# Expert routing beside the matmuls: new reckoned times, a wider wait, a gate on the search, row tiles one by one

## Chip, cores and metric

One core of one Trainium2 chip. The metric is the device time of one launch in microseconds (us). Three runs of the kernel before took 701.67, 702.32 and 698.46 us; the median is 701.67.

## What is computed

The kernel takes a windowed attention with a few global rows (8 batches, 8 heads, 512 local and 32 global rows, head size 64), lays its output out as 4608 rows of 512, and puts these through a layer of 8 experts. The experts are the part that matters here:

```python
logits = x @ w_gate
flat = logits.flatten()
order = np.argsort(-flat)
for idx in order:
    tok, e = (int(idx) // E, int(idx) % E)
    if assigned[tok] >= 0 or counts[e] >= cap:
        continue
    assigned[tok] = e
    counts[e] += 1
for e in range(E):
    mask = assigned == e
    h = np.maximum(x[mask] @ w1[e], 0.0)
    out[mask] = h @ w2[e]
```

Each expert gets exactly 576 rows (`cap`). Which expert is full next, and which rows it gets, is known only after a search over all logits that are still open.

## The kernel before

**Stages.** Attention runs first and writes the rows `xd` to memory. Then phase 0 of the routing runs alone. From 247.2 us on, eight experts follow one another, in the order in which the routing finds them full.

**One expert** (`ffn`, line 1096). All products are done in three fp32r parts: high x high, high x low, low x high. Part H is 16 groups of 12 matmuls, 128x272 each, of the weights `w1h`/`w1l` with the rows `xh`/`xl` (line 1119). After each group ScalarE writes `hh` and VectorE the remainder `hl`. Part Y begins with `rest_out` (line 1086, the last 32 rows) and goes on with four tiles of 128 rows in `rows_out` (line 1077, 24 matmuls of 128x512 each). When `rest_out` has been issued, `mid[0]` is set to the number of the expert. Beside an expert the inputs of the next are made ready: `get_w1` and `get_w2` gather its weights (GpSimd, by `widx`), `get_x` gathers its rows (by `idx`), `split_w1`, `split_w2` and `trans_x` (line 956) split them into the high part (ScalarE) and the low part (VectorE). `trans_x` first turns a tile of 128 rows on TensorE. Weights of the next expert come into the same tiles, so half of w1 may be split only after `f` is 4, and the rest only after `mid`.

**One routing phase** (`phase`, line 736, with `setup` and `search`, line 679). `setup` makes the keys, then the search does eight turns. A turn counts with 18 small matmuls into `A`, scales by `ce` on VectorE, sums with two matmuls, finds the bound by a scan (`pm`), lowers (`lower`) and compares again (`cand`, which writes `G`). From the eighth scan come `widx` (the next expert) and, after a prefix sum and one-hot products, `idx` (its rows). Phase `ph` serves expert `ph`, and runs beside the experts before it. Phase 7 has no search.

**The planner.** The order on each engine's queue is set when the kernel is built, by reckoned times. `step(ns)` (line 1016) is called after each large matmul and moves TensorE's reckoned time `V.now` on. `Queue` (line 527) adds a cost to `V.busy`, the reckoned time at which VectorE is through, for each operation issued (line 548). `mm` (line 626) does the small matmuls: it moves `V.now`, and sets `V.busy` to at least a little after it. In `chain` (line 991) the phases are generators: each yields the reckoned time from which it may go on, or -1, at which waiting `hl` operations (`fill`, by `bubble`) are issued first. Before a small matmul that reads a VectorE result it yields `ready()`, which is `V.busy` and a margin, `HOP`. `step` takes the first entry of `todo` whose time has come and whose condition holds (the gathers, splits, turned tiles and scatters), lets the routing go on, and issues one waiting low part (`lows`) when VectorE is nearly through. Low parts wait for 900 ns (`LOW`) after their high part, those of row tiles for 1500 (`TURN`). `calm` is: fewer than two low parts waiting. At the end of an expert, what is not yet ready is waited for with steps of 120 ns and no matmul.

The reckoned time is used for nothing but the order: on the chip each instruction waits for its data by semaphores.

Of the kernel before, what the change touches and what calls it, by code (L numbers as in the profile page):

```python
# [510 lines left out]
TX = 22000  # L511
TW = 34000
AHEAD = 200
HOP = 400
SLACK = 100
PACE = 250
CU = 64
# [9 lines left out]
class Queue:  # L527


    def __init__(s, eng):  # L530
        s.eng = eng
        s.now = s.busy = 0.0

    def ready(s):
        return s.busy + HOP

    def pace(s):
        return s.busy - PACE
# [1 line left out]
    def __getattr__(s, name):  # L540
        op = getattr(s.eng, name)

        def issue(*args, **kw):
            aps = [x for x in list(args) + list(kw.values()) if hasattr(x, "dtype") and hasattr(x, "shape")]
            n = max(int(np.prod(x.shape[1:])) for x in aps)
            fast = name in ("tensor_scalar", "tensor_copy") or name == "tensor_tensor" and all(
                mybir.dt.size(x.dtype) == 2 for x in aps)
            s.busy = max(s.busy, s.now) + 150 + n * (2.1 if "scan" in name else 1.9 if name == "transpose" else 0.55 if fast else 1.05)
            return op(*args, **kw)  # L549
        return issue  # L550


class Routing:
# [69 lines left out]
    def begin_ps(s, ctx):  # L623
        s.ps = ctx.enter_context(s.tc.tile_pool(name="rps", bufs=1, space=PSUM))

    def mm(s, out, *args, ns=60, **kw):
        s.nc.tensor.matmul(out, *args, **kw)  # L627
        s.V.now += ns
        s.V.busy = max(s.V.busy, s.V.now + 200)

    def t(s, name, shape, dt=F32):
        return s.sb.tile([128] + shape, dt, name="r_" + name)
# [16 lines left out]
    def lower(s, P, it):  # L649

        y = s.t("z%d" % (it % 2), [34], BF16)
        s.V.scalar_tensor_tensor(y, s.x, P, s.dg[:, it - 1], op0=ALU.subtract, op1=ALU.add)
        s.x = y

    def key(s, j):
# [23 lines left out]
    def search(s):  # L679
        nc = s.nc  # L680
        for it in range(NIT):
            yield -1
            yield s.when
            A = s.ps.tile([128, 2, E], F32, name="R")
            for i in range(18):
                j, r = slice(2 * i, 2 * i + 2), 32 * (i % 4)
                g, o = (s.G[:, i].rearrange("p a b -> p (a b)"), s.oh[:, j]) if i < 17 else (s.one[:, :32], s.rem[:, :2])
                s.mm(A[r:r + 32], g, o, ns=20, start=(i < 4), stop=(i >= 14))
            p = s.ps.tile([128, 16, E], F32, name="R2")
            if it == 0:  # L690
                s.digits(slice(0, 34))
                s.x = s.y0
            ce = s.t("ce", [2, 16, E], F16)
            s.V.tensor_tensor(ce, A[:, :, None, :].to_broadcast([128, 2, 16, E]),
                              s.dk[:, :, :, None].to_broadcast([128, 2, 16, E]), op=ALU.mult)
            when = s.V.ready()
            yield -1
            yield when
            for k in range(2):
                s.mm(p, s.big, ce[:, k], start=(k == 0), stop=(k == 1))  # L700
            pm = s.t("pm%d" % (it % 2), [16 * E])
            s.V.tensor_tensor_scan(pm, p.rearrange("p a b -> p (a b)"), s.fin[:, it], 0.0, op0=ALU.max,
                                         op1=ALU.min)
            P = pm[:, 16 * E - 1:16 * E]
            if it < NIT - 1:
                s.lower(P, it + 1)
                s.cand(s.x, s.step2[:, it + 1])
        s.P = P.bitcast(I32)
# [27 lines left out]
    def phase(s, ph):  # L736
        nc = s.nc
        last = ph == E - 1
        S = s.t("S", [68], BF16)
        vs = s.ix.tile([128, 1], F32, name="vs")  # L740
        if not last:
# [15 lines left out]
        a = s.t("a", [34])  # L757
# [21 lines left out]
        p = s.ps.tile([128, 68], F32, name="R")  # L779
# [42 lines left out]
        rhs = s.rhs  # L822
# [15 lines left out]
        p = s.ps.tile([128, 64], F32, name="R2")  # L838
        for j in range(34):
            r = 32 * (j % 4)  # L840
            s.mm(p[r:r + 32], rhs[:, j // 2, :, :, j % 2].rearrange("p a b -> p (a b)"), ohl[:, j // 2, :, j % 2], ns=20, start=(j < 4),
                 stop=(j >= 30))
        if more and ph:
            pg = s.ps.tile([128, E], F32, name="R")
# [48 lines left out]
def experts(ctx, tc, A, xd, ident, rt, out):  # L893
# [62 lines left out]
    def trans_x(xg, t):  # L956
        n = sizes[t]
        flush(1)
        p = ps.tile([128, 4, 128], F32, name="H", bufs=3)
        for d in range(4):  # L960
            nc.tensor.transpose(p[:, d, :n], xg[t][:n, 128 * d:128 * d + 128], ident[:n, :n])  # L961
        q = slice(128 * t, 128 * t + n)
        if rt.beside:
            split(xh[:, :, q], xl[:, :, q], p[:, :, :n], V, TURN)
        else:
            nc.scalar.activation(xh[:, :, q], p[:, :, :n], AF.Copy)
            V.tensor_tensor(xl[:, :, q], p[:, :, :n], xh[:, :, q], op=ALU.subtract)
# [23 lines left out]
    def chain():  # L991
        for ph in range(1, E):
            if 1 < ph < E - 1:
                yield from rt.setup(slice(0, 34))
            yield from rt.phase(ph)

    routing = chain()

    def bubble():
        while fill:  # L1000
            fill.pop(0)()

    def at(tag, t, f, cond=None):
        todo.append((tag, t, cond, f))
# [11 lines left out]
    def step(ns):  # L1016
        V.now += ns
        for i, (tag, t, cond, f) in enumerate(todo):
            if t <= V.now and (cond is None or cond()):
                todo.pop(i)  # L1020
                f()
                break
        while not done[0] and V.now >= need[0]:
            v = next(routing, None)
            if v is None:
                done[0] = True
            elif v < 0:
                bubble()
            else:
                need[0] = v  # L1030
        if lows and lows[0][0] <= V.now and V.busy < V.now + AHEAD:
            lows.pop(0)[1]()
        if V.busy < V.now and (done[0] or need[0] > V.now + SLACK):
            bubble()
# [16 lines left out]
    def get_x(p):  # L1051
        flush()
        xg = load_x(p)
        for t in range(5):
            r = pool_op(1040, sizes[t] * 2048)
            at(f"x{p}", r + (900 if p == 1 else 0), lambda t=t: trans_x(xg, t), lambda: mid[0] == p - 1)

    def get_w2(p):
        flush()
# [17 lines left out]
    def rows_out(ph, t):  # L1077
        p = ps.tile([128, DM], F32, name="Y", bufs=3)
        q = slice(128 * t, 128 * t + 128)
        for f in range(8):  # L1080
            for k, (h, w) in enumerate(((hh, w2h), (hh, w2l), (hl, w2h))):
                nc.tensor.matmul(p, h[:, f, q], w[f], start=(f + k == 0), stop=(f + k == 9))  # L1082
                step(216)
        out_tile(ph, t, p)

    def rest_out(ph):
# [9 lines left out]
    def ffn(ph):  # L1096
        nxt = ph + 1
        t0 = V.now
        cur[0] = ph
        half = []  # L1100
        if nxt < E:
            at(f"g{nxt}", t0, lambda: get_w1(nxt, half), lambda: nxt in rt.widx and not pending(f"b{ph}"))
            at(f"h{nxt}", t0, lambda: get_x(nxt), lambda: nxt in rt.idx and (mid[0] == ph or V.now > t0 + TX))
            at(f"v{nxt}", t0, lambda: get_w2(nxt), lambda: mid[0] == ph and nxt in rt.widx and
               (not pending(f"h{nxt}") or V.now > t0 + TW))
        for f in range(8):
            if f == 4:
                force(f"b{ph}")
                half.append(True)
                if ph == E - 1:  # L1110
                    force("out")
                    nc.gpsimd.drain()
            for hf in range(2):
                q = slice(HF * hf, HF * hf + HF)
                p = ps.tile([128, HF], F32, name="H", bufs=3)
                fs = slice(128 * f, 128 * f + 128)
                for d in range(4):
                    for k, (w, x) in enumerate(((w1h, xh), (w1h, xl), (w1l, xh))):
                        nc.tensor.matmul(p, w[d][:, fs], x[:, d, q], start=(d + k == 0), stop=(d + k == 5))  # L1119
                        step(117)  # L1120
                nc.scalar.activation(hh[:, f, q], p, AF.Relu)  # L1121
                if hf:
                    nc.scalar.activation(h32[:, f], p[:, HF - 32:HF], AF.Relu)  # L1123
                while fill:
                    fill.pop(0)()
                fill.append(lambda p=p, f=f, q=q: V.scalar_tensor_tensor(
                    hl[:, f, q], p, 0.0, hh[:, f, q], op0=ALU.max, op1=ALU.subtract))

        while fill:
            fill.pop(0)()  # L1130
        force(f"w{ph}")

        for part in (0, 1, 2, 3, 4) if ph == E - 1 else (4, 0, 1, 2, 3):
            if part == 4:
                rest_out(ph)
            else:
                rows_out(ph, part)
        while nxt < E and (pending(f"g{nxt}", f"h{nxt}", f"a{nxt}", f"x{nxt}", f"v{nxt}") or lows or nxt not in raw1):
            step(120)
            bubble()  # L1140
# [127 lines left out]
```

## Time and profile before

| | |
|---|---|
| median of three runs | 701.67 us (698.46 to 702.32) |
| profiled execution | 703.93 us, span 702.0 us |
| TensorE (PE) busy | 651.6 us, 93% of the span |
| VectorE (DVE) busy | 460.5 us, 66% |
| ScalarE (ACT) busy | 308.9 us, 44% |
| GpSimd (POOL) busy | 247.8 us, 35% |
| chain that ended last | TensorE 88%, VectorE 5%, issue 3%, DMA 2% |

The span runs from the first to the last instruction; the execution's own time is 1.9 us more. Times in rows are us from the start of the span. A row in order of time has the start, the length, the engine, the line, the operation, out<-in, the shapes, the count, and in brackets the engine's idle time before it with what ended that. All VectorE operations of the planner have line 549 (the helper that records them), and its small matmuls line 627, so they are told apart by tile. Matmuls are pipelined: the length of one is longer than the step from one to the next.

### The profile page before, as it was taken

How to read it: one execution, taken by the hardware profiler on the slowest of the kernel's cores; microseconds unless marked ns; L12 is line 12 of the kernel's file. 1: busy time of each engine (PE TensorE's matmuls, PEld its weight loads, DVE VectorE, ACT ScalarE, POOL GpSimd, SP SyncE). 2: the span in 40 equal slices, each digit the busy share in tenths (PEclk: the TensorE clock that was granted, in tenths of full speed). 3: DMA queues.
4: the chain of work that ended last, by engine and by line, in shares of the span. 5: the costliest groups of instructions: out<-in, count | busy, mean ns of one | idle time of the engine just before them, and what ended most of it. 6: DMA issues, size and time to landing. Idle time of an engine off the chain costs nothing.

```text
span 702.0 us, 24724 instructions
## 1 busy us (share of the span) xinstructions
PE 651.6 (93%) x10364; PEld 547.5 (78%) x10364; DVE 460.5 (66%) x1765; ACT 308.9 (44%) x828; POOL 247.8 (35%) x313
## 2 busy tenths in 40 slices
PE   7878989889992799989999999999999999999996
PEld 6666767677781699769879878978987987988985
DVE  4678777777876787687767767767776764640510
ACT  5776767776840253233324334333333332641410
POOL 4686658766610410430241141152132034412001
PEclk9999999999995599989999999999999999999999
DMA  8676767776310530630361361343135045631001
GB/s 256 198 222 198 225 209 233 240 218 207 111 67 2 184 122 5 252 113 1 129 203 39 125 197 49 121 127 122 44 132 179 17 145 197 207 128 46 16 15 50
DMA packets 41119, 93.91 MB, mean 134 GB/s; under 512 B 5424, under 2 KB 28208, under 8 KB 36912
## 3 DMA queue, kind: packets, MB, share of 16 engines
q0 software_dynamic: 10240, 51.39, 21.1%
q1 hardware_dynamic: 30768, 40.95, 19.2%
q8 instruction: 81, 1.33, 0.8%
q14 instruction: 30, 0.25, 0.1%
HBM read 74.49 MB, written 17.83 MB: 132 GB/s over the span
## 4 chain that ended last, share of the span: by engine, by line
PE 88%; DVE 5%; issue 3%; DMA 2%; ACT 1%; SPq 0%; POOLq 0%; ACTq 0%
PE H L1119 28%; PE Y L1082 27%; PE T L90 11%; PE S L90 7%; PE O L90 7%; PE R L627 4%; PE H L961 3%; PE Y L1090 2%; DVE r_pm L549 1%; DMA xg<-xd,idx 1%; DVE r_G L549 1%; DMA mask<-in_mask_dram 1%; DMA qk<-in_qk_dram 1%; DVE r_ce L549 0%; DMA out_dram<-y,idx 0%
## 5 line engine op out<-in xcount | busy, mean ns | idle before, releaser
L1119 PE MATMUL H<-xh,w1h 128*128 128x272 f32 x512 | 153.3, 299 | 1.4 <-DVE hl L549 1.3
L1119 PE MATMUL H<-xh,w1l 128*128 128x272 f32 x512 | 150.0, 293 | 0.0
L1119 PE MATMUL H<-xl,w1h 128*128 128x272 f32 x512 | 149.6, 292 | 0.0
L971 POOL DMA_INDIRECT out_dram<-y,idx x40 | 42.5, 1062 | 199.7 <-ACT y L1070 111.3
L1121 ACT ACTIVATE hh<-H 128x272 fp32r<-128x272 f32 x128 | 50.9, 398 | 127.5 <-PE H L1119 115.7
L1082 PE MATMUL Y<-w2h,hh 128*128 128x512 f32 x256 | 103.5, 404 | 0.0
L1082 PE MATMUL Y<-w2l,hh 128*128 128x512 f32 x256 | 103.2, 403 | 0.0
L1082 PE MATMUL Y<-w2h,hl 128*128 128x512 f32 x256 | 103.0, 402 | 0.0
L1119 PEld LDWEIGHTS H<-xh,w1h 128*128 128x128 f32 x512 | 97.4, 190 | 3.4 <-DVE hl L549 2.5
L1119 PEld LDWEIGHTS H<-xl,w1h 128*128 128x128 f32 x512 | 97.4, 190 | 0.2
L1119 PEld LDWEIGHTS H<-xh,w1l 128*128 128x128 f32 x512 | 97.2, 190 | 0.2
L126 POOL COPY vw<-vw 32x650 f32<-32x650 f32 x96 | 69.3, 722 | 59.0 <-DMA vw<-in_vw_dram 37.2
L180 ACT ACTIVATE p<-p,nm 128x128 f32<-128x128 f32 x256 | 78.0, 396 | 8.1 <-DVE nm L175 8.1
L1070 ACT ACTIVATE y<-Y 128x512 f32<-128x512 f32 (+1 forms) x40 | 21.4, 535 | 119.9 <-PE Y L1082 87.2
L175 DVE CUSTOM_DVE_ANT_0 p<-S,mask 128x128 f32<-128x128 f32 x256 | 56.5, 286 | 25.3 <-PE S L90 24.4
L549 DVE SCALAR_TENSOR_TENSOR hl<-H,hh 128x272 fp32r<-128x272 f32 x128 | 54.8, 434 | 26.3 <-ACT h L1123 16.8
L90 PE MATMUL S<-qk 64*32 64x128 f32 (+2 forms) x2240 | 53.2, 294 | 9.4 <-issue 6.8
L549 DVE TENSOR_TENSOR w2l<-w2r,w2h 128x512 fp32r<-128x512 f32 x64 | 42.9, 683 | 23.8 <-ACT w2h L929 23.8
L913 POOL DMA_INDIRECT xg<-xd,idx x40 | 42.8, 1071 | 42.1 <-DVE idx L549 29.0
L1082 PEld LDWEIGHTS Y<-w2h,hh 128*128 128x128 f32 x256 | 48.2, 188 | 10.3 <-issue 1.2
L1082 PEld LDWEIGHTS Y<-w2h,hl 128*128 128x128 f32 x256 | 48.1, 188 | 9.7
L1082 PEld LDWEIGHTS Y<-w2l,hh 128*128 128x128 f32 x256 | 48.3, 188 | 9.4
(175 smaller groups left out, 1130.5 us busy)
## 6 DMA issues: line engine op xcount, KB each, us to landing
qk<-in_qk_dram SPq DMA_DIRECT2D x64, 204.0 KB, 3.7
vw<-in_vw_dram SPq DMA_DIRECT2D x64, 162.5 KB, 3.5
xd<-xs SPq DMA_DIRECT2D x28, 256.0 KB, 3.5
qk<-in_qk_dram SPq DMA_DIRECT2D x32, 200.0 KB, 3.8
xd<-xs SPq DMA_DIRECT2D x1, 1024.0 KB
xg<-xd,idx POOLq DMA_INDIRECT x40, 3.6
out_dram<-y,idx POOLq DMA_INDIRECT x40, 2.8
vw<-in_ve_dram SPq DMA_DIRECT2D x32, 16.2 KB, 3.4
```

The costliest lines, as they stand in the source:

```text
L90: s.last = op(o, w, x, **kw)
L126: copy(bv[32 * g:32 * g + 32], av[32 * g + 32:32 * g + 64])
L175: nc.vector.tensor_tensor_reduce(s.p[:, c, :], s.st[:, c, :], mask[:, c, :], -SCALE, BIG, ALU.add, ALU.min, s.nm[:, c:c + 1])
L180: nc.scalar.activation(s.p[:, c, :], s.p[:, c, :], AF.Exp, bias=s.nm[:, c:c + 1], scale=-1.0)
L549: return op(*args, **kw)
L627: s.nc.tensor.matmul(out, *args, **kw)
L913: nc.gpsimd.indirect_dma_start(out=dst, out_offset=None, in_=src, element_offset=off, in_offset=bass.IndirectOffsetOnAxis(ap=idx, axis=0))
L971: nc.gpsimd.indirect_dma_start(out=out4 if t == 4 else out, out_offset=bass.IndirectOffsetOnAxis(ap=rt.idx[ph][:, k:k + 1], axis=0), in_=y ...
L1070: nc.scalar.activation(y, p[:, :w], AF.Copy)
L1082: nc.tensor.matmul(p, h[:, f, q], w[f], start=(f + k == 0), stop=(f + k == 9))
L1119: nc.tensor.matmul(p, w[d][:, fs], x[:, d, q], start=(d + k == 0), stop=(d + k == 5))
L1121: nc.scalar.activation(hh[:, f, q], p, AF.Relu)
```

## The change

The reckoned costs change: a VectorE operation has 60 ns instead of 150 beside its elements (a scan 190, and `lower` 190 more), an H matmul 124 instead of 117, a Y matmul 230 instead of 216, the small matmuls 23, 90 and 17, and the time from a small matmul to VectorE is 150 or nothing instead of 200. The margin `HOP` becomes `s.hop`: 280 (`SOON`) for phases 0 and 1 and 800 from phase 2 on. A phase is begun only when `rest_out` of the expert two back has been issued; until then the chain yields every 300 ns of reckoned time. Before a waiting low part is issued, waiting `hl` operations are. A row tile is turned only when no low part is waiting.

```diff
-HOP = 400
+SOON = 280
+HOP = 800
...
+        s.hop = SOON
 
     def ready(s):
-        return s.busy + HOP
+        return s.busy + s.hop
...
-            s.busy = max(s.busy, s.now) + 150 + n * (2.1 if "scan" in name else 1.9 if name == "transpose" else 0.55 if fast else 1.05)
+            s.busy = max(s.busy, s.now) + (190 if "scan" in name else 60) + n * (
+                2.1 if "scan" in name else 1.9 if name == "transpose" else 0.55 if fast else 1.05)
...
-    def mm(s, out, *args, ns=60, **kw):
+    def mm(s, out, *args, ns=60, lag=150, **kw):
         s.nc.tensor.matmul(out, *args, **kw)
         s.V.now += ns
-        s.V.busy = max(s.V.busy, s.V.now + 200)
+        s.V.busy = max(s.V.busy, s.V.now + lag)
...
         s.V.scalar_tensor_tensor(y, s.x, P, s.dg[:, it - 1], op0=ALU.subtract, op1=ALU.add)
+        s.V.busy += 190
...
-                s.mm(A[r:r + 32], g, o, ns=20, start=(i < 4), stop=(i >= 14))
+                s.mm(A[r:r + 32], g, o, ns=23, lag=-50, start=(i < 4), stop=(i >= 14))
...
-                s.mm(p, s.big, ce[:, k], start=(k == 0), stop=(k == 1))
+                s.mm(p, s.big, ce[:, k], ns=90, start=(k == 0), stop=(k == 1))
...
         last = ph == E - 1
+        s.V.hop = HOP if ph > 1 else SOON
...
-            s.mm(p[r:r + 32], rhs[:, j // 2, :, :, j % 2].rearrange("p a b -> p (a b)"), ohl[:, j // 2, :, j % 2], ns=20, start=(j < 4),
+            s.mm(p[r:r + 32], rhs[:, j // 2, :, :, j % 2].rearrange("p a b -> p (a b)"), ohl[:, j // 2, :, j % 2], ns=17, start=(j < 4),
...
             if 1 < ph < E - 1:
                 yield from rt.setup(slice(0, 34))
+            while mid[0] < ph - 2:
+                yield V.now + 300
             yield from rt.phase(ph)
...
         if lows and lows[0][0] <= V.now and V.busy < V.now + AHEAD:
+            bubble()
             lows.pop(0)[1]()
...
-            at(f"x{p}", r + (900 if p == 1 else 0), lambda t=t: trans_x(xg, t), lambda: mid[0] == p - 1)
+            at(f"x{p}", r + (900 if p == 1 else 0), lambda t=t: trans_x(xg, t), lambda: mid[0] == p - 1 and not lows)
...
-                step(216)
+                step(230)
...
-                        step(117)
+                        step(124)
```

## Rows read from the trace of the kernel before

**Rows 1.** The page: granted clock in 40 equal slices of the span.

```profile
PEclk9999999999995599989999999999999999999999
```

**Rows 2.** Experts 0, 1, 3, 6: length, busy (count) by engine, PEclk, DMA, GB/s.

```profile
247.23:310.42 63.19, 59.64 (x639) 50.97 (x638) 49.06 (x140) 24.41 (x58) 16.38 (x15) 0.97 0.38 132
310.42:368.55 58.13, 58.07 (x571) 49.73 (x572) 41.48 (x120) 18.69 (x46) 13.48 (x13) 0.97 0.31 106
...
425.45:482.80 57.35, 56.92 (x575) 48.51 (x575) 40.64 (x118) 20.62 (x51) 15.11 (x14) 1.00 0.34 115
...
596.80:647.52 50.72, 50.72 (x374) 45.63 (x374) 19.43 (x37) 20.06 (x50) 13.37 (x14) 1.00 0.38 132
...
sum 446.67, PE 441.78 PEld 382.23 DVE 279.65 ACT 159.16 POOL 107.98; mean PE 55.22 PEld 47.78 DVE 34.96 ACT 19.90 POOL 13.50
```

**Rows 3.** The same view, two stretches at the seam of experts 0 and 1.

```profile
302.00:308.30 6.30, 3.12 (x59) 2.33 (x58) 5.05 (x13) 4.89 (x11) 3.24 (x3) 0.89 0.31 101
308.30:313.60 5.30, 5.01 (x40) 4.54 (x40) 3.75 (x10) 0.91 (x2) 0.97 (x1) 0.50 0.27 100
```

**Rows 4.** TensorE in order of time there: start, length, instruction, [idle before].

```profile
304.79 0.99 PE L961 MATMUL H<-ident,xg 128*128 128x128 f32 x8 [1.28 <-DVE xl L549]
...
307.28 0.30 PE L627 MATMUL R<-r_oh,r_G 128*32 128x16 f16 x17 [1.28 <-DVE r_G L549]
```

**Rows 5.** GpSimd in order of time: first gathers of w1, x; last of w2.

```profile
284.38 0.96 POOL L913 DMA_INDIRECT w1r<-in_w_dram,widx  x1 [5.41 <-DVE r_a L549]
...
288.24 0.96 POOL L913 DMA_INDIRECT w2r<-in_w_dram,widx  x1 [0.31 <-issue]
...
295.86 1.30 POOL L913 DMA_INDIRECT xg<-xd,idx  x1 [5.32 <-DVE idx L549]
```

**Rows 6.** VectorE in order of time: start of search 1 and its first scan.

```profile
249.18 0.44 DVE L549 TENSOR_TENSOR r_oh<-r_v,r_mo 128x272 f16<-128x272 bf16 x1
...
254.03 0.42 DVE L549 TENSOR_TENSOR_SCAN r_pm<-R,fin 128x128 f32<-128x128 f32 x1 [1.17 <-PE R L627]
```

**Rows 7.** VectorE in order of time: last scan of search 1 to idx.

```profile
283.06 0.42 DVE L549 TENSOR_TENSOR_SCAN r_pm<-R,fin 128x128 f32<-128x128 f32 x1 [1.02 <-PE R L627]
...
293.22 0.29 DVE L549 TENSOR_TENSOR r_w<-R,cf 128x128 bf16<-128x128 f32 x1 [2.23 <-PE R L627]
...
295.42 0.17 DVE L549 CAST idx<-R 128x5 int32<-128x5 f32 x1 [1.12 <-PE R L627]
```

**Rows 8.** VectorE in order of time beside expert 4.

```profile
485.48 0.43 DVE L549 SCALAR_TENSOR_TENSOR hl<-H,hh 128x272 fp32r<-128x272 f32 x1
485.83 0.68 DVE L549 TENSOR_TENSOR w2l<-w2r,w2h 128x512 fp32r<-128x512 f32 x1
486.44 0.42 DVE L549 TENSOR_TENSOR_SCAN r_pm<-R,fin 128x128 f32<-128x128 f32 x1
486.90 0.25 DVE L549 SCALAR_TENSOR_TENSOR r_z<-r_z,r_pm,r_dg 128x34 bf16<-128x34 bf16 x1
...
490.54 0.42 DVE L549 TENSOR_TENSOR_SCAN r_pm<-R,fin 128x128 f32<-128x128 f32 x1
...
519.02 0.17 DVE L549 CAST idx<-R 128x5 int32<-128x5 f32 x1 [1.11 <-PE R L627]
```

**Rows 9.** TensorE beside expert 4: around one counting block; its one wait.

```profile
488.42 0.29 PE L1119 MATMUL H<-xh,w1l 128*128 128x272 f32 x1
...
489.08 0.29 PE L1119 MATMUL H<-xl,w1h 128*128 128x272 f32 x1
...
505.88 0.39 PE L1119 MATMUL H<-xh,w1h 128*128 128x272 f32 x1 [0.43 <-DVE hl L549]
```

**Rows 10.** Chain of waits in order of time: `rest_out` of expert 4.

```profile
510.81 1.88 PE Y L1090 x64
```

**Rows 11.** TensorE beside Y of expert 3: first and last row tile turned.

```profile
466.07 0.60 PE L961 MATMUL H<-ident,xg 128*128 128x128 f32 x4
...
472.25 0.43 PE L961 MATMUL H<-ident,xg 32*128 32x32 f32 x4
```

## The prediction

> **What bounds the kernel now.** I read the stretches by expert first. From the first matmul of H of expert 0 to the last of Y of expert 7 the kernel takes 446.67 us, of which TensorE is busy for 441.78, so TensorE bounds it and idles for 4.89 us in all [rows 2]. Expert 6, beside which no search runs, takes 50.72 us; expert 3, with a whole routing phase beside it, takes 57.35; experts 0 and 1 take 63.19 and 58.13 [rows 2]. Every expert has the same matmuls, so the two first ones are where something is lost. The short stretches show it: in the 6.3 us from 302.0 TensorE is busy for only 3.12, then 5.01 of 5.3 us at a granted clock of 0.50, the 1.2 GHz level; the page's clock row has no other slice below 8 after the routing of expert 0 than this one place [rows 1, 3]. So the seam costs 3.18 + 0.29 = 3.47 us of idle time, and half of 5.01 = 2.5 us of slow clock: 6.0 us together. That is most of what there is: 4.89 + 2.5 = 7.4 us.
>
> Why there: TensorE had finished Y of expert 0 and waited for VectorE, 1.28 us for an `xl` (the row tiles of expert 1 were still being split) and 1.28 for a search step of phase 2 that stood behind such splits [rows 4]. The splits were late because `idx` was: it came at 295.42, and the first gather of rows went out at 295.86, after both w1 and w2 (w1 at 284.38, the last of w2 at 288.24) [rows 5, 7]. `idx` was late because search 1 was slow: its one-hot operand was ready at 249.62, yet the first scan ran at 254.03, and the last of the eight at 283.06, 4.15 us for each turn; after it `r_w` stood 2.23 us for TensorE, which was held back by the planner's reckoning, not by data [rows 6, 7]. In the later experts the order fits: one wait of 0.43 us for an `hl` beside expert 4 [rows 9].
>
> **The reckoned times.** The planner adds 150 ns to each VectorE operation. Starts against starts show what one really takes when the next stands behind it: the `hl` 0.35 us (the new constants give 60 + 272 x 1.05 = 346), `w2l` 0.61 (598), the scan 0.46 (459) [rows 8]. So about 90 ns an operation were reckoned too many. The counting block of 18 matmuls stretches one H interval of about 0.125 to 0.66 - 0.125 = 0.53, so 0.41 of its own [rows 9]; the new 18 x 23 is 414. No instruction is added or removed by this: the same work is put in another order. Before H of expert 0 the order does not depend on the planner, so all of the first 247 us stays.
>
> **Search 1 with a margin of 280.** One turn by the new costs: 280 + 414 (count) + 329 (`ce`) + 280 + 180 (sum) + 150 + 459 (scan) + 286 + 359 (compare) = 2.74 us, and on average half a matmul step at each of two waits, 0.12. VectorE's own share of a turn is 1.43; two `hl` (0.70) and one to two weight splits (0.6 each) also run in it, so it fills at about 3.3 us, the value I take, between 2.86 and the 4.15 of now. The start gains some 1.2 (about fifteen operations at 90 ns ahead of the first count), so the last scan moves from 283.06 to about 249.2 + 2.9 + 7 x 3.3 = 275.3. From there to `idx` are 12.4 us and some 25 operations; 2.2 us of it go with the 90 ns: `idx` at about 285.5, ten earlier. TensorE does not get faster by that, but the rows of expert 1 go out ten earlier too.
>
> **The price of the short margin.** Sixteen waits now stand on 0.28 us instead of 0.40 and on honest costs. The result of an operation lies there 0.08 after the next may start (0.43 against 0.35 [rows 8]), so about 0.2 is left for the way to TensorE and for errors. The planner knows no wait of VectorE for ScalarE; where an `hl` stands in front of a search step, it can be late. Bounds: nothing, or 16 times the one wait that the steady part shows, 0.43 [rows 9], so 6.9 us. I take 0.8 (four waits of 0.2), near the lower end, because the costs now fit the rows.
>
> **The seam, with rows turned singly.** Y of expert 0 now ends at about 302.0 [rows 3]; with the row tiles of expert 1 turned inside it instead of behind it (some 2 us of TensorE) it ends at about 304. Rows gathered from 285.5 on, behind w1 and w2 on the same DMA engines, are there by about 296. The new condition lets a tile be turned only when no split is pending; five tiles took 6.2 us for four steps in the steady part, about 1.55 each, and that already was one `xl` at a time [rows 11]. Eight w1 splits first, then 5 x 1.6 = 8 us, so the last is done a little before Y ends. I take all 6.0 us as gained; the bounds are 3.0 (rows land late) and 6.0. With TensorE no longer idle, nothing lets its clock fall.
>
> **Wide margin and gate from phase 2 on.** The turn becomes 2.74 + 2 x 0.52 + 0.12 = 3.9 us; now it is 4.10 [rows 8]. So the search keeps its pace, and its waits get more cover: this hides the jitter at no cost. The gate holds search `ph` until `rest_out` of expert `ph`-2 is out. While it holds, only the routing chain waits; VectorE and TensorE queues get other work, no instruction stands in line. Now `idx` of phase 5 comes 519.02 - 510.81 = 8.2 us after the start of `rest_out` of expert 4 [rows 8, 10]. With the gate at `rest_out` of expert 3, some 57 us earlier [rows 2], 8 x 3.9 = 31 for the search and 13 for the rest (12.4 in [rows 7]) bring it at about +44, so 13 us before the point at which rows may be turned. That is earlier than now, not later. What can be gained there is the waits of 0.43 beside experts 3, 4 and 5; I take 0.6 of 1.3, since a burst of small operations after the search still stands in front of an `hl`.
>
> **Sum.** 6.0 + 0.6 - 0.8 = 5.8 us. The profiled execution took 703.93 with a span of 702.0, 2.3 above the median of 701.67; I take the difference from the median: 695.9 us. What this kernel's runs can tell from no change is about 0.5%, so 698.2 and 705.2 are the limits.
>
> **Rivals.** (a) *The margin is too short.* TensorE waits at most of the 16 steps of search 1, for 0.43 as in [rows 9]: 701.67 - 6.6 + 6.9 = 702.0. For it speaks that waits for ScalarE are not reckoned. Against it, that [rows 8] fit the costs. Chance 0.12. The Trainium skill, "VectorE: DVE Perf Modes", section "The DRAIN you can't avoid", says that after a Vector operation the next does not start until the pipe is empty; by that an operation would cost its full duration, the new constants would be some 85 ns short each time, and this rival would come true. Here the `hl` of 0.43 us lets the next start after 0.35, so the trace speaks against it. (b) *The transfers close the seam only half.* w2 is still sent ahead of the rows, since 34 us into the expert its turn comes, as in [rows 5]; the rows land late and half of the seam stays: 701.67 - 3.0 = 698.7. Chance 0.12. (c) *Slower.* The margin of 800 makes the search late: if a turn beside a busy VectorE took over 5.5 us instead of 3.9, `idx` would come 13 us later, after the rows must be turned, and the tiles, now one by one, would end after Y. Each of four more seams would then look like [rows 3], 6.0 each: 701.67 - 6.6 + 24 = 719. Against it, the turn of 4.10 now, with reckoned costs that were too high [rows 8]. Chance 0.08. (d) *Nothing comes of it.* VectorE's own load, not the margin, sets the turn of search 1; `idx` stays near 295 and the seam with it: 701.7. For it, VectorE is busy for 49.06 of 63.19 us beside expert 0 [rows 2]; against it, the 2.23 us of waiting in [rows 7]. Chance 0.06.
>
> **Numbers.** The forecast has 0.62, with 692.5 to 698.2 as its own range: the lower end is all the visible loss and a little of what the rows do not resolve (701.67 - 7.4 - 1.8). Faster is the forecast and most of (b), with what of (a) stays mild: 0.70. Same is (d), the rest of (b) and most of (a): 0.20. Slower is (c) and the worst of (a): 0.10. The range goes up to 701.5, leaving out (c), (d) and half of (a).
>
> **What would show it.** Right: the first scan of search 1 at about 252, the last at 275 to 277, `idx` at 285 to 288; no slice with the clock below 1.00 between 300 and 316; experts 0 and 1 together about 6 us shorter than 121.3; turns of about 3.9 us from phase 2 on, beginning at `rest_out`. Wrong: waits of TensorE for `r_G` or `r_ce` beside expert 0 that add up to several us (a); the last turned tile after the last matmul of Y (b, c).

## The result and the profile after

The changed kernel takes 711.0 us (709.9 to 711.65, four runs), the kernel before 702.0 us: ratio 1.0136, 95% interval 1.0097 to 1.0175 (the chip of these runs is not on record). It is slower by 1.4% where 695.9 us was forecast. In three later groups of runs, each on a chip of its own, the ratio was 1.0098 to 1.0156.

Until phase 1 ends, the profile after (execution 710.38 us, span 708.6) follows the forecast. H of expert 0 starts at 242.88, 4.35 us earlier than in the trace before, so 4.35 us are to be added for comparing. VectorE in order of time: first and last scan of search 1, `idx` of expert 1; then TensorE's last turned tile and the first matmul of H of expert 1; then the page's clock row.

```profile
248.16 0.42 DVE L552 TENSOR_TENSOR_SCAN r_pm<-R,fin 128x128 f32<-128x128 f32 x1
...
271.54 0.42 DVE L552 TENSOR_TENSOR_SCAN r_pm<-R,fin 128x128 f32<-128x128 f32 x1
...
282.02 0.16 DVE L552 CAST idx<-R 128x5 int32<-128x5 f32 x1 [0.21 <-PE R L630]
...
301.85 0.43 PE L966 MATMUL H<-ident,xg 32*128 32x32 f32 x4
...
303.87 0.29 PE L1127 MATMUL H<-xh,w1h 128*128 128x272 f32 x1
```

```profile
PEclk9999999999985699999999999999999999999999
```

Moved by 4.35 that is 252.5, 275.9 and 286.4, against 252, 275 to 277 and 285 to 288. The last tile is turned inside Y, H follows without a gap, and the slice with 8 that [rows 1] has at the seam is gone; the three low ones left are the routing ahead of the experts. The time is lost later. The stretches by expert, columns as in [rows 2]:

```profile
242.88:304.04 61.16, 59.93 (x656) 49.71 (x657) 51.41 (x147) 22.54 (x54) 16.31 (x15) 1.00 0.38 137
304.04:367.30 63.26, 60.47 (x616) 48.89 (x616) 43.87 (x128) 20.71 (x50) 13.52 (x14) 1.00 0.30 103
367.30:427.93 60.63, 58.31 (x596) 48.38 (x596) 41.18 (x121) 20.61 (x50) 13.80 (x14) 1.00 0.31 108
427.93:487.50 59.57, 57.38 (x577) 48.10 (x576) 40.48 (x118) 20.46 (x50) 14.19 (x14) 1.00 0.33 109
487.50:548.38 60.88, 58.61 (x576) 49.27 (x575) 40.98 (x120) 20.39 (x50) 14.06 (x14) 0.97 0.31 107
...
sum 457.62, PE 445.49 PEld 378.93 DVE 279.75 ACT 158.62 POOL 105.08; mean PE 55.69 PEld 47.37 DVE 34.97 ACT 19.83 POOL 13.14
```

The experts take 457.62 us instead of 446.67 [rows 2], 10.95 more. Expert 0 gained 2.0, expert 1 lost 5.1, expert 3 lost 2.2. TensorE is idle for 457.62 - 445.49 = 12.1 us instead of 4.9; the other 3.7 us are in its busy time, which the waits do not cover. The four longest of its waits, over all experts (us, times, longest):

```profile
PE H L1127 <- DVE hl L552: 6.2, 5, 1.9
PE Y L1098 <- issue: 1.9, 5, 0.5
PE R L630 <- DVE r_ce L552: 1.3, 3, 0.6
PE R L630 <- DVE r_ohl L552: 1.0, 1, 1.0
...
```

Two losses show. **First, `hl`**: 6.2 us, where the kernel before has 1.3 in three waits of 0.4, one of them in [rows 9]. VectorE in order of time at the start of H of expert 3, from the eighth scan of the search on, and the TensorE row that waits:

```profile
432.17 0.42 DVE L552 TENSOR_TENSOR_SCAN r_pm<-R,fin 128x128 f32<-128x128 f32 x1
432.62 0.15 DVE L552 TENSOR_SCALAR r_vi<-r_pm 128x1 int32<-128x1 int32 x1
...
434.00 1.29 DVE L552 TENSOR_TENSOR w2l<-w2r,w2h 128x512 fp32r<-128x512 f32 x2
...
435.42 1.11 DVE L552 SCALAR_TENSOR_TENSOR hl<-H,hh 128x272 fp32r<-128x272 f32 x3
```

```profile
435.89 0.40 PE L1127 MATMUL H<-xh,w1h 128*128 128x272 f32 x1 [1.33 <-DVE hl L552]
```

Ten small operations in a row (432.62 to 434.0) and two `w2l`, which `get_w1` issues by `flush()` as soon as `widx` is there, stand ahead of three `hl`; H has three buffers in PSUM, so TensorE stops. In the trace before, the same burst is later in its H, which begins at 425.45 [rows 2], and no split stands between it and the `hl`:

```profile
447.04 0.21 DVE L549 TENSOR_SCALAR widx<-vs,cf 128x1 int32<-128x1 f32 x1
...
448.04 0.78 DVE L549 SCALAR_TENSOR_TENSOR hl<-H,hh 128x272 fp32r<-128x272 f32 x2
```

In the changed kernel, beside expert 4, such a wait (1.85 us) even costs the clock: TensorE is busy for 1.75, then 1.40 of 2.5 us, and after that the granted clock is 0.50, the 1.2 GHz level.

```profile
492.50:495.00 2.50, 1.75 (x14) 1.53 (x13) 2.40 (x14) 1.22 (x4) 0.98 (x1) 1.00 0.00 0
495.00:497.50 2.50, 1.40 (x9) 1.43 (x10) 2.50 (x7) 0.00 (x0) 1.35 (x1) 0.90 0.72 233
497.50:500.00 2.50, 2.50 (x14) 2.38 (x13) 2.22 (x12) 0.40 (x1) 0.00 (x0) 0.50 0.90 321
```

**Second, gathers beside small matmuls.** First expert 2 in the trace before: its `rest_out` (64 matmuls, 1.95 us from the first start to the last end in every expert), then, well apart, its row gathers, the last gather of w2 and the first counting block of a search:

```profile
396.08 1.96 PE L1090 MATMUL Y<-w2r,h 128*32 128x128 f32 x64
...
398.10 0.28 ACT L1070 ACTIVATE y<-Y 128x128 f32<-128x128 f32 x1 [1.43 <-PE Y L1090]
...
404.79 1.30 POOL L913 DMA_INDIRECT xg<-xd,idx  x1 [4.91 <-DVE idx L549]
...
413.03 0.94 POOL L913 DMA_INDIRECT w2r<-in_w_dram,widx  x1 [0.30 <-issue]
...
414.42 0.17 PE L627 MATMUL R<-rem,one 128*32 128x16 f16 x1
414.90 0.42 DVE L549 TENSOR_TENSOR r_ce<-R,dk 128x256 f16<-128x256 f32 x1 [1.86 <-PE R L627]
```

In the changed kernel, `rest_out` of expert 1 and the row gathers, which `idx` at 332.33 released:

```profile
332.46 2.03 PE L1098 MATMUL Y<-w2r,h 128*32 128x128 f32 x55
332.74 0.95 POOL L918 DMA_INDIRECT xg<-xd,idx  x1 [9.00 <-DVE idx L552]
...
334.83 0.43 PE L1098 MATMUL Y<-w2r,h 128*32 128x128 f32 x5 [0.34 <-issue]
...
337.06 0.27 PE L1098 MATMUL Y<-w2r,h 128*32 128x128 f32 x1 [0.47 <-issue]
...
341.53 0.28 ACT L1078 ACTIVATE y<-Y 128x128 f32<-128x128 f32 x1 [8.47 <-remote]
```

TensorE waits for nothing that the profile shows ("issue"), `rest_out` takes 4.9 us, and ScalarE gets its result 4.2 us after the end of the last matmul. "remote" says that the semaphore waited for rose only then, with no row of an engine ending there: ScalarE was free, and word of the result came late. Nor was TensorE short of instructions as far as the trace shows, since no packet of an instruction queue lies between 332 and 342. The same happens to the first counting block of a search, now right behind `rest_out` and beside the gathers of w2:

```profile
398.41 0.95 POOL L918 DMA_INDIRECT w2r<-in_w_dram,widx  x1 [2.68 <-ACT h L1131]
...
399.22 0.17 PE L630 MATMUL R<-rem,one 128*32 128x16 f16 x1
...
401.28 0.42 DVE L552 TENSOR_TENSOR r_ce<-R,dk 128x256 f16<-128x256 f32 x1 [2.43 <-remote]
```

`r_ce` begins 1.9 us after the block it waits for has ended, where it was 0.3 in the trace before; in the first turns of two later searches that follow `rest_out` it is 2.2 and 2.0 us. (Behind `rest_out` of expert 1 it is 1.9 us too, but there VectorE itself is busy until then.)

### The profile page after: what moved, and what is told of

It reads as the page before. It is cut to its first block, busy times and chain, and to the rows that moved or that the text cites. A ratio compares the mean times of both kernels' runs of the same rounds, so it can differ in the third digit from the quotient of the medians.

```text
span 708.6 us, 24727 instructions
## 1 busy us (share of the span) xinstructions
PE 651.5 (92%) x10364; PEld 541.6 (76%) x10364; DVE 460.4 (65%) x1765; ACT 307.9 (43%) x828; POOL 245.1 (35%) x313
## 4 chain that ended last, share of the span: by engine, by line
PE 81%; DVE 9%; issue 4%; DMA 2%; another core or an unknown queue 1%; ACT 1%; SPq 0%; POOLq 0%; ACTq 0%
PE Y L1090 25%; PE H L1127 24%; PE T L90 11%; PE S L90 7%; PE O L90 7%; PE R L630 4%; PE H L966 3%; DVE w2l L552 2%; DVE hl L552 1%; PE Y L1098 1%; DVE r_pm L552 1%; DVE r_ce L552 1%; DMA qk<-in_qk_dram 1%; DMA xg<-xd,idx 1%
## 5 line engine op out<-in xcount | busy, mean ns | idle before, releaser
L1127 PE MATMUL H<-xh,w1h 128*128 128x272 f32 x512 | 150.1, 293 | 6.9 <-DVE hl L552 6.2
L1090 PE MATMUL Y<-w2h,hh 128*128 128x512 f32 x256 | 105.1, 411 | 0.2 <-issue 0.2
L976 POOL DMA_INDIRECT out_dram<-y,idx x40 | 39.3, 982 | 190.3 <-ACT y L1078 143.3
L918 POOL DMA_INDIRECT xg<-xd,idx x40 | 41.2, 1030 | 65.7 <-DVE idx L552 40.7
```

The lines of the kernel that those rows point to most:

```text
L918: nc.gpsimd.indirect_dma_start(out=dst, out_offset=None, in_=src, element_offset=off, in_offset=bass.IndirectOffsetOnAxis(ap=idx, axis=0))
L976: nc.gpsimd.indirect_dma_start(out=out4 if t == 4 else out, out_offset=bass.IndirectOffsetOnAxis(ap=rt.idx[ph][:, k:k + 1], axis=0), in_=y ...
```

## Experiments

Theory A: the searches end too early, in the stretch of H in which w2 is split, and their rows and counting blocks meet gathers. Rivals: the gathers are innocent and all of it is the order on VectorE (B), the new costs or the single rows lose by themselves (C), the wide margin does (D), the gate does (E). The runs of one group (a "call" in the expectations) share a chip and the runs of the kernel before; ratios are to these. "Late results" ("late signals" in the expectations) are results of TensorE that reach ScalarE or VectorE long after the last matmul's row has ended.

**First group: one part undone at a time.** `glate` begins a search 12 us after `rest_out`, about where the kernel before has it; `xlate` keeps the rows until `rest_out` is issued; the others undo the margin and the gate.

```diff
# glate (rest[0] is V.now when mid[0] is set)
-            while mid[0] < ph - 2:
+            while mid[0] < ph - 2 or ph > 1 and V.now < rest[0] + 12000:
# xlate
- ... lambda: nxt in rt.idx and (mid[0] == ph or V.now > t0 + TX))
+ ... lambda: nxt in rt.idx and mid[0] == ph)
# hop400
-HOP = 800
+HOP = 400
# nogate
-            while mid[0] < ph - 2:
-                yield V.now + 300
```

> The changed kernel, but the row gathers of the next expert go out only after rest_out (not already 22 us into the expert); all else stays. Theory A (search ends too early: its burst of small VectorE operations and the forced w2 low parts stand in front of an hl, about 7.5 us of TensorE waits for hl; and the early row gathers, running beside rest_out's dense small matmuls, hold up the instruction supply, about 4 us): the gap of rest_out of expert 1 and the 'issue' waits go, the hl waits stay near 6 us in the PE waits; 706 to 708. Theory B (row gathers are innocent; all of the loss is in the order on VectorE): 710 to 712, gaps of 'issue' still there. Theory C (the new constants or the singly turned rows cost by themselves, wherever the search stands): 710 to 712.

> The changed kernel with the gate 12 us later: search ph begins 12 us after rest_out of expert ph-2 instead of at it, which is where the kernel before has it; margin 800, costs and single rows stay. Theory A: search end, idx and w1 gather return to some 15 to 29 us into the expert, no w2 splits stand there: hl waits in the PE waits fall from 6.2 to under 2 us, no gap in rest_out; 696 to 701, the seam gain of about 6 us kept. Theory C (constants, margin or single rows cost by themselves): 707 to 712 with the waits moved, not gone.

> The changed kernel with margin 400 instead of 800 from phase 2 on; gate stays. The search ends about 1 us into H, before most w2 splits, and the row gathers stand 22 us into H. Theory A: the burst now stands in the first two H tiles beside fewer w2 splits: hl waits 2 to 5 us instead of 6.2, 704 to 709. Theory D (the wide margin itself is what costs): below 702. Theory C: 710 or more.

> The changed kernel without the gate. The searches then drift earlier from expert to expert (search 3 begins in H of expert 2, search 5 runs inside H of expert 4), so their ends meet the w2 splits beside expert 3 only and no routing is left beside experts 5 and 6. Theory A: hl waits 3 to 5 us instead of 6.2, 705 to 710. Theory E (the gate itself is the loss): under 702.

Measured on chip 1: `glate` 696.97 us, 0.9928 (0.9889 to 0.9968); `nogate` 698.46, 0.9952 (0.9926 to 0.9978); `xlate` 701.02, 0.9987 (0.9956 to 1.0018); `hop400` 703.06, 1.004 (1.0001 to 1.0079). Moving the gate alone gives most of the forecast gain, so the costs, the wide margin and the single rows do no harm in that order: C falls. `hop400` is not under 702, as D wanted, but just below what A gave it; `nogate` lies where E wanted it, and `xlate` is 10 below the 711, where A gave at most 5. No run of the four showed late results, and the changed kernel itself did not run on chip 1, so what each part alone costs there is not known.

**Second group: again, and single parts.**

```diff
# singleonly: the kernel before with
- ... lambda: mid[0] == p - 1)
+ ... lambda: mid[0] == p - 1 and not lows)
# nosingle: the changed kernel with the line above undone
# costs: the changed kernel without gate and single rows, and
-SOON = 280
-HOP = 800
+SOON = 400
+HOP = 400
```

> The changed kernel itself once more, beside the others. In its profile ACT and DVE got TensorE's results 0.3 to 4 us late in many places (y of rest_out 4.2 us behind the last matmul of expert 1, r_ce about 2 us behind the counting block of three later searches), also beside expert 0, where the run with the later row gathers has the very same order and shows no such lateness. Theory F (that lateness is not the kernel's but of that one call): H waits for hl of about 6 us, no late r_ce, 704 to 707. Theory G (it belongs to this order of gathers): 709 to 712 again.

> The kernel before with the new reckoned times alone: margin 400 throughout, no gate, rows turned as before. The searches then drift early from expert to expert, the end of search 5 meets the first quarter of H of expert 4. Theory A: part of the seam after expert 0 closes, experts 0 and 1 together 118 to 120 us, and hl waits of 2 to 5 us come back later: 698 to 702. Rival (the costs alone give the whole gain): below 697.

> The kernel before with only the rows turned singly (no tile while a split is pending). Theory A: idx of expert 1 stays late, the seam stays open, about 6 us, and nothing else changes: 700 to 704. Rival (single rows slow the turning down and open the seam further): over 705.

> The changed kernel without the singly turned rows. Theory A: the search still ends 2 to 5 us into H among the w2 splits: hl waits 4 to 6 us; about the time of the changed kernel in the same call, within 3 us. Rival (the single rows cause the waits): hl waits under 2 us, at least 5 us below the changed kernel.

Measured on chip 3: the changed kernel 713.47 us, 1.0152 (1.0102 to 1.0203), its late `r_ce` in the same places as before; `costs` 729.35, 1.037 (1.0317 to 1.0423); `singleonly` 715.87, 1.0152 (1.0082 to 1.0222); `nosingle` 717.85, 1.0226 (1.0181 to 1.027). Three expectations missed, `costs` and `singleonly` by far, and all to the slow side; `singleonly` lies where its rival put it. It shows why its part is worth something only with an early `idx`: with `idx` still late (295.52) the five tiles are turned one by one from 306.7 to 312.6, behind the last matmul of Y at 301.54, and H of expert 1 starts at 314.23. That makes expert 0 5.8 us longer than in the trace before; the rest of its 13.5 us is in the later experts, where first counting blocks stand beside gathers and `r_ce` starts up to 2.3 us late. Beside the early `idx` the same line gains 4.4 us (`nosingle` against the changed kernel). `costs` lost most by late `r_ce` (7.0 us of waits) and `xl` (5.0). All four showed late results, so whether the chip or the order makes them was open.

**Third group: the same kernels on one chip.**

> The changed kernel, on one chip with three of its variants that ran elsewhere before. Theory H (the late signals go with the chip or the call, not with the order): this kernel and its variants show them alike in this call, all or none; if none, this kernel takes 702 to 706, if all, 710 to 714. Theory I (they go with the order of this kernel): 710 to 714 with r_ce about 2 us late in three searches, while the three variants of this call show none.

> The changed kernel with the row gathers only after rest_out, again. Theory I: 699 to 703, no late signals, as in its first run. Theory H: as the changed kernel of this call shows; with late signals 706 to 712.

> The changed kernel with the gate 12 us later, again. Theory I: 695 to 699, no late signals. Theory H: with late signals 702 to 710.

> The changed kernel without the gate, again. Theory I: 696 to 701. Theory H: with late signals 705 to 720, as the kernel with the costs alone, which drifts in the same way, gave 729.

Measured on chip 0: changed kernel 712.03 us, 1.0098 (1.0062 to 1.0135); `xlate` 710.09, 1.0089 (1.0056 to 1.0123); `nogate` 720.56, 1.0215 (1.0134 to 1.0295); `glate` 699.24, 0.9932 (0.9898 to 0.9966). Neither H nor I is right alone, and E falls with `nogate`: the group on chip 1 forgives orders that those on chips 0 and 3 do not. Each chip ran in one group only, so chip and group cannot be told apart. One kernel (`xlate`), the same `rest_out` of expert 1, on chip 1 and on chip 0:

```profile
332.31 1.96 PE L1098 MATMUL Y<-w2r,h 128*32 128x128 f32 x64
332.59 0.95 POOL L918 DMA_INDIRECT xg<-xd,idx  x1 [9.00 <-DVE idx L552]
...
334.33 0.28 ACT L1078 ACTIVATE y<-Y 128x128 f32<-128x128 f32 x1 [1.43 <-PE Y L1098]
```

```profile
335.17 2.02 PE L1098 MATMUL Y<-w2r,h 128*32 128x128 f32 x55
335.46 0.95 POOL L918 DMA_INDIRECT xg<-xd,idx  x1 [9.01 <-DVE idx L552]
...
337.50 0.43 PE L1098 MATMUL Y<-w2r,h 128*32 128x128 f32 x5 [0.31 <-issue]
...
344.12 0.28 ACT L1078 ACTIVATE y<-Y 128x128 f32<-128x128 f32 x1 [8.36 <-remote]
```

The gather starts 0.3 us into `rest_out` in both (set later in the queues, it still waits for `idx` alone). On chip 1 all 64 matmuls run through and ScalarE starts 0.06 us behind them; on chip 0 nine are left over, and ScalarE starts 4.9 us late. The experts take 446.3 and 454.9 us. In `glate` on chip 0 `idx` comes 2 us later against `rest_out`, the gathers begin as it ends, and `y` is on time, though beside expert 0 this run has late results too (`y` of `rest_out` 1.6 us); these rows are of that run:

```profile
337.32 1.08 PE L1098 MATMUL Y<-w2r,h 128*32 128x128 f32 x32
...
338.49 1.05 PE L1098 MATMUL Y<-w2r,h 128*32 128x128 f32 x32
339.53 0.95 POOL L918 DMA_INDIRECT xg<-xd,idx  x1 [8.15 <-DVE idx L552]
339.61 0.28 ACT L1078 ACTIVATE y<-Y 128x128 f32<-128x128 f32 x1 [0.26 <-PE Y L1098]
```

**Fourth group: gathers or small matmuls (J or K), and the w2 splits.**

```diff
# gate6: as glate, with
+ ... V.now < rest[0] + 6000:
# w2keep: low parts of w2 are marked; in get_w1
-        flush()
+        while any(not x[2] for x in lows):
+            lows.pop(0)[1]()
# dummyx: glate, and at the start of rest_out
+        if 0 < ph < E - 1:
+            for t in range(4):
+                nc.scalar.activation(spare[t][:, 0:1], h32[:, 7, 0:1], AF.Copy)
+                gather(spare[t], xd, 0, rt.idx[ph][:, t:t + 1])
```

> The changed kernel as the mark for this call: 709 to 714 with late signals from TensorE (as on three chips so far), or 702 to 706 without them.

> The changed kernel with the gate 6 us later (half of what the fast variant has). The w2 gathers, issued in the 3.5 us behind rest_out, are then over before the first counting block of a search. Theory J (TensorE's small matmuls, the counting block or rest_out, report late when GpSimd issues gathers beside them): r_ce no longer 2 us late behind rest_out of experts 2 to 4, but rest_out of expert 1 still beside row gathers, and the hl waits still 4 to 6 us since the search ends 7 us into H: 4 to 6 below the changed kernel. Theory K (many small matmuls one after another are late by themselves): as J here, but then the next run is unlike.

> The changed kernel, where the w1 gather pushes only pending w1 low parts ahead of it, no longer the w2 low parts. Theory A (these w2 low parts and the burst stand in front of three hl): hl waits fall by about 1.2 us in each of experts 2 to 5 where two low parts stood there, from 6.5 to 3 or less: 3 to 4 below the changed kernel. Rival (the burst of small operations alone makes the wait): hl waits stay at 5 us or more, time within 1.5.

> The fast variant (gate 12 us later) with four row gathers into spare tiles added to each of experts 1 to 6, released by the last h and so issued beside rest_out, which nothing else is there; they are extra work, and nobody reads them. Theory J: y of rest_out comes 2 to 5 us late there, rest_out itself shows gaps of issue, 4 to 12 above the fast variant's 697 to 699. Theory K: y stays within 0.1 us of the last matmul, time within 2 of 697 to 699 (the real row gathers are 4 us later, which Y of 20 us covers).

Measured on chip 9: changed kernel 712.25 us, 1.0156 (1.0087 to 1.0224); `gate6` 714.91, 1.0187 (1.0108 to 1.0267); `w2keep` 711.35, 1.0141 (1.0066 to 1.0215); `dummyx` 727.41, 1.0284 (1.0179 to 1.039). `w2keep` brought the `hl` waits from 6.7 us in 7 to 5.1 in 8, less than half of the fall that A gave it, and the time fell by 0.9 us; both lie where the rival put them, so the burst makes most of the wait, the pushed splits the rest. `dummyx` decides nothing by its time, since the real rows came so late that TensorE waited 14.4 us for them. Its rows speak for J: one added gather starts beside each `rest_out`, and `y` comes 1.2 to 1.9 us late in experts 1 to 5 and 4.9 in expert 6, where K gave 0.1 and `glate` on chip 0 has 0.07. `rest_out` itself shows no gap there, against J. `gate6` missed in an instructive way. Its late `r_ce` were gone and its `hl` waits down to 2.3 us, below the 4 to 6 expected, but its row gathers had moved from H onto `rest_out` of all of experts 1 to 5, which took 3.5 to 5.3 us each.

**Fifth group: the gathers alone.** `gate6` again (`gate6b`), and `gate6x`, where the rows wait in the planner until the scatter of `rest_out`'s `y` has been issued, and so stand behind it in GpSimd's queue.

```diff
- ... (mid[0] == ph or V.now > t0 + TX)
+ ... (mid[0] == ph and not pending("out") or V.now > t0 + TW)
```

> The kernel with the gate 6 us later once more, as the mark for the next: 711 to 717 with rest_out of experts 1 to 4 at 4.6 to 5.2 us instead of 1.9, as before; on a chip that does not show late signals at all, 698 to 703.

> The same kernel, where the row gathers stand behind the scatter of rest_out's y in GpSimd's queue, so that no gather is issued while TensorE runs rest_out; the search stays where it is. Theory J (gathers beside rest_out make TensorE wait and its results late): rest_out back at 1.9 to 2.2 us in every expert, issue waits under 1 us, 11 to 14 below the run beside it, so 699 to 704. Theory K (the early search or the small matmuls themselves): issue waits and time within 3 of the run beside it.

Measured on chip 5: 712.56 us, 1.0123 (1.0067 to 1.0178), and 706.85, 1.0042 (1.0004 to 1.0079). `rest_out` of expert 2, first `gate6b`, then `gate6x`:

```profile
398.81 1.85 PE L1098 MATMUL Y<-w2r,h 128*32 128x128 f32 x40
399.35 0.95 POOL L918 DMA_INDIRECT xg<-xd,idx  x1 [0.30 <-issue]
...
402.41 0.66 PE L1098 MATMUL Y<-w2r,h 128*32 128x128 f32 x14 [0.29 <-issue]
```

```profile
391.16 1.95 PE L1098 MATMUL Y<-w2r,h 128*32 128x128 f32 x64
393.18 0.28 ACT L1078 ACTIVATE y<-Y 128x128 f32<-128x128 f32 x1 [1.37 <-PE Y L1098]
393.74 1.00 POOL L976 DMA_INDIRECT out_dram<-y,idx  x1 [14.66 <-ACT y L1078]
...
400.28 0.17 PE L630 MATMUL R<-rem,one 128*32 128x16 f16 x1
...
403.73 0.42 DVE L552 TENSOR_TENSOR r_ce<-R,dk 128x256 f16<-128x256 f32 x1 [6.49 <-PE H L966]
```

With the gathers out of the way `rest_out` is back at 1.95 us in experts 1 to 5, from 3.2 to 4.5, and the waits for issue ahead of its matmuls, 4.6 us in all, are gone. J holds for `rest_out`. The time fell by 5.7 of the 11 to 14 expected, because the gathers now stand beside the first counting block, whose `r_ce` starts 3.3 us late; TensorE waits 4.3 us for `r_G` and 2.5 for `r_ce` in its place. The loss moves with the gathers.

## Why the prediction was wrong

**Search 1, its price and the seam: right.** The scans and `idx` came to within 1 us of the forecast. For the short margin 0.8 was taken; beside expert 0 no wait for `r_G` or `r_ce` exists, and one of 1.0 us for `r_ohl`, so rival (a) is out. ("No other slice below 8" misreads [rows 1]: the slice at the seam is an 8, and behind the routing of expert 0 no other is below 9.) The seam was sized at 6.0: experts 0 and 1 take 116.65 and 117.4 us in the two runs of `glate` against 121.32 [rows 2], a gain of 4.7 and 3.9 where 6.0 - 0.8 = 5.2 was forecast; in the changed kernel, with the losses below, they take 124.42. Rows landed in time, so (b) is out, and (d) with it.

**The step that failed is "Wide margin and gate from phase 2 on".** It says that the wide margin "hides the jitter at no cost", that under the gate "no instruction stands in line", and of `idx` "That is earlier than now, not later", and it stops there: lateness alone was priced. The turn was nearly right (4.2 us, the mean from 402.82 to 432.17 for seven, instead of 3.9), and `idx` of expert 4 came 9.4 us ahead of `rest_out`, where 13 were forecast. Right, and worth less than nothing. Starting at `rest_out`, the search ends with its burst in the first quarter of H, beside the w2 splits, where the kernel before had it 21.6 us into H (`widx` of phase 4 at 447.04, H of expert 3 from 425.45); its first counting block meets the w2 gathers; and the early `idx` sends the rows out beside `rest_out`. In the trace before the first and the last of these pairs do not meet, and the second only just: the block stands 0.3 us behind the last w2 gather's row, and `r_ce` comes 0.3 us late. In place of a free, earlier search the runs showed a kernel 8.1 to 11.1 us slower than the one before, and on chip 0 moving the gate by 12 us takes all of it away and leaves a gain of 4.7. The step even named the burst ("a burst of small operations after the search still stands in front of an `hl`") but only as what limits a gain of 0.6.

**The sum, with measured terms.** On chip 1, which shows no late results, `glate` is 4.2 us below the kernel before (701.18 - 696.97), and `xlate` 4.05 above `glate`, with 5.1 instead of 2.1 us of `hl` waits: that is about what the search's early end costs. On chip 0 `xlate` is 6.1 above the kernel before, on chip 1 0.2 below it: 6.3 for the late results. The changed kernel is 1.9 above `xlate` on chip 0. -4.2 + 4.05 + 6.3 + 1.9 = 8.1, and 712.03 - 703.97 = 8.1 was measured. The sum closes by the way it is built and proves nothing; that the 6.3 are late results is read from the rows of `xlate` on the two chips, and the 1.9 are not explained. The forecast of -5.8 for everything but the search's place was thus 1.1 to 1.6 too large. The 0.6 from the steady part did not come: experts 2 to 4 take 57.6 us each in `glate`, with one `hl` wait of 0.69 us in each.

**Rival (c)** was the only one clearly on the slow side, and had the sign of the cause wrong: it made the search too late. The rule of the Trainium skill quoted with rival (a) ("VectorE: DVE Perf Modes", "The DRAIN you can't avoid") does not bear on the result. That section adds that a next operation that is not held starts earlier; here the three `hl` at 435.42 again take 1.11 us together, not three times 0.43.

**A version that beats both.** `glate`, the changed kernel with the gate 12 us later, is at 0.993 on both chips where it ran: 4.2 and 4.7 us below the kernel before, and on chip 0 12.8 below the changed kernel beside it.

## What to carry to other kernels

An earlier result is not a free result: list what it releases, and look at what stands in that place on every engine, the queue of the gathers too. When a chain that runs beside other work is moved, its start, its end and its burst each get a new neighbour; check all three against the trace before. A variant that looks harmless on one chip should be timed on a second before it is trusted.

## What was not expected of the hardware

Indirect gathers issued by GpSimd disturb blocks of many small matmuls, though the two share no data: `rest_out` went from 1.95 to between 2.5 and 5.3 us, and results reached ScalarE or VectorE up to 5.5 us late. H and Y, with 0.12 and 0.23 us a matmul, lost only 0.3 and 0.8 us to such gaps in the whole trace of the changed kernel, though most gathers stand beside them, but a result of H can be late as well: in this row `hh` starts 1.9 us after its group's last matmul has ended (393.69), with row gathers at 392.36 and 393.61.

```profile
395.61 0.40 ACT L1129 ACTIVATE hh<-H 128x272 fp32r<-128x272 f32 x1 [2.91 <-remote]
```

Four chips (0, 3, 5, 9) showed it in every run with that order, chip 1 in none, and the kernel before, which keeps the two mostly apart, was at 701.2 to 704.7 us on all five. What is shared, and what differs in chip 1 or its group, is open. The Trainium skill, "Perfetto Trace Analysis", "Summary: the profiler window per engine type", says that TensorE's end in a trace is an estimate and that the spreading of a semaphore is in no row; so these traces cannot tell whether the sums were late in PSUM or only the news of them. The gaps in `rest_out` itself are starts of matmuls, and these the rows do show.
